# Batch 1's first transform stage on folded inputs, and the last quarter of w_in converted at the turn to the MLP

## The chip, the cores and the metric

The kernel runs on one core of a Trainium2 chip. The metric is the device time of one execution in microseconds (us). The core has five engines that run side by side, each through its own list of instructions in a fixed order: TensorE (PE; its weight loads are listed as PEld), VectorE (DVE), ScalarE (ACT), GpSimd (POOL) and SyncE (SP). DMAs are issued from the lists of SP and ScalarE.

## What is computed

For x of 8 batches x 3008 rows x 256 columns: a real FFT over the rows, a complex linear layer with bias on the 256 columns, a soft threshold of real and imaginary part apart, the inverse FFT, and then a two-layer MLP (256 to 2048 to 256) over all 24064 rows.

```python
X = np.fft.rfft(x, axis=1)                      # x: 8 x 3008 x 256
Yr = Xr @ w_r - Xi @ w_i + b_r
Yi = Xr @ w_i + Xi @ w_r + b_i
Yr = np.sign(Yr) * np.maximum(np.abs(Yr) - 0.01, 0.0)      # Yi alike
y = np.fft.irfft(Yr + 1j * Yi, n=3008, axis=1)
h = y.reshape(24064, 256) @ w_in                # w_in: 256 x 2048
out = np.maximum(0.01 * h, h) @ w_out           # w_out: 2048 x 256
```

The weights of the MLP arrive as 64-bit floats, read as pairs of 32-bit words.

## The kernel before

3008 is 47 x 64, so the FFT is done as products with small constant matrices. Per batch the work has these parts.

- Stage A (`fwd`): the 47-point transform. x comes as two halves, xa (row n) and xb (row -n). The cosine half needs xa + xb and the sine half xa - xb; making them is a fold. The columns are cut in seven groups c, six of 512 and one of 256; per group there are two results (h = 0, 1), which ScalarE copies from PSUM and which a DMA writes to `u_dram`. Batch 0 folds on VectorE, batches 2 to 7 fold on GpSimd (L245, L246). Batch 1 (`stage_a1`) doesn't fold: it makes each result from two products, with xa and with xb, using a third constant, the negated sine matrix (`fa32[:, 2]`); that is four products per group.
- The middle stage (`mid`): for 12 pairs j, a load of u, the 64-point transform (L343), a copy and sum ef (L347, L348), the linear layer (products into `pso` for the part kc, into `psf` for the rest), the bias sum on GpSimd (`kb = bias + kc`, L377, one buffer), then on VectorE t = psf + kb (L385), the clamp c (L386) and t - c (L387), then zf (four instructions on ScalarE, L391 and L395; for the last pair two of them on VectorE, L393), a product with zf (`stage_g`), a copy v and its write to `v_dram` (L415).
- The inverse (`inverse`): V is loaded (`vin`, L454), multiplied (L475), copied to odd (L478), combined on VectorE (L479, L481) and put in order in yc (L488). `forms` makes the sums of a seven-product scheme and splits each into a high and a low part (L500, L501) for one chunk of 512 rows, so an fp32-like product is three fast ones.
- The MLP (`moe`): 47 chunks x 8 steps q. A step has `moe_a` (products into `psh`, sums on VectorE, L538 to L541), `moe_b` (more products, L551 to L558 make g and split it into gh and gl) and, two steps later, `moe_o` (products with w_out into `pso`).

Both weights must be converted from 64-bit floats and split. w_in goes in quarters (`convert_win`, work tiles cva, cvq, ws), each with thirteen VectorE instructions, from `float64_parts` (L131 to L137) to the splits (L171, L172). w_out goes in eight chunks (`load_wout`; raw, then cva in tag "zf", L131 to L137 and L200 to L202); the first two raw loads are early, the other six use the two buffers "e" and "z" in turn. Step q of the first chunk of rows needs w_out chunk q two steps later.

The start of the program is: stage A of batch 0, quarters 0 and 1 of w_in, then the middle stage of batch 0 with quarters 2 and 3 of w_in and the x loads of batch 1 among it; then the turn: V of batch 0 is read back and inverted for the first chunk while TensorE does stage A of batch 1, five of its seven groups; the last two groups (c = 4, 5) come in the first MLP steps. From there on the MLP runs, with stage A and the middle stages of later batches in between.

The order of the instructions on each engine is made by a scheduler that goes by the order in which the program issues them and by a model of the engines. `tc.issue_after(x)` only says that an instruction is placed after x; it adds no wait by itself. Tiles with one tag share that tag's buffers in the order of their allocation, so a new tile waits for the last reader of the old one.

Of the kernel before, what the change touches and what calls it, by code (L numbers as in the profile page):

```python
# [8 lines left out]
F32 = mybir.dt.float32  # L9
# [11 lines left out]
P = 128  # L21
PA = NK1 * NG
# [8 lines left out]
def spectral_mlp_kernel(  # L31
# [125 lines left out]
    def convert_win(c):  # L157


        a, q, s = win_tmp  # L160
        float64_parts(win_raw[c], a, q)
        dve.tensor_add(a, a, q)
        a = a.rearrange("p (j q i m) -> p j q i m", j=NH, q=2, i=2)
        a11, a12, a21, a22 = (a[:, j, :, i] for i in range(2) for j in range(2))
        dve.tensor_add(s[:, 0], a21, a22)
        dve.tensor_sub(s[:, 2], a11, a21)
        dve.tensor_sub(s[:, 1], s[:, 0], a11)
        dve.tensor_sub(s[:, 3], a12, s[:, 1])
        hi, lo = (w[:, :, 2 * c:2 * c + 2] for w in consts["win"])
        for k, w in ((slice(0, 2), a[:, :, :, 0]), (2, a22), (slice(3, 7), s)):  # L170
            act.copy(hi[:, k], w)  # L171
            last = dve.tensor_sub(lo[:, k], w, hi[:, k].bitcast(F32))  # L172
        return last
# [36 lines left out]

    reads, written, turned, turning, thresholded = [], [], [], [], []
    NX = -(-NS // 2)
# [3 lines left out]
    def fwd(b):  # L216
# [5 lines left out]
        def load(c):  # L222
            cols = slice(2 * c * D, min(2 * c + 2, NS) * D)
            n = cols.stop - cols.start
            if b < NPRE:
                tag, bufs = (XT, XT1)[b][c]
                x2 = sb.tile([PA, 2, 2 * D], F32, name="xin", tag=tag, bufs=bufs)
                x_t[c] = [x2[:, h, :n] for h in range(2)]
            else:
                x_t[c] = [  # L230
                    sb.tile([PA, 2 * D], F32, name=f"xin{h}", tag="uv"[h], bufs=3 - h)[:, :n] for h in range(2)
                ]
# [25 lines left out]
        def stage_a(c, h):  # L258
# [9 lines left out]
            if b == 0:  # L268
                written.append(st)

        def stage_a1(c):

            n = x_t[c][0].shape[1]
            pas = [(bank("psf", 2) if c in (4, 5) else bank("psh", 4))[:PA, :n] for _ in range(2)]
            for h in range(2):
                with tc.issue_after(turning[NPAIR - 2].ins):
                    products(pas[h], [
                        (consts[f"fa{h}32"], (x_t[c][0],)), (consts[f"fa{2 * h}32"], (x_t[c][1],))])
            for h in range(2):
# [3 lines left out]
        if b == 1:  # L283
            for c in range(NX):
                load(c)
                yield 0
            for c in (0, 1, 2, 3, 6, 4, 5):
                stage_a1(c)
                yield 6 * x_t[c][0].shape[1]
# [22 lines left out]
    def mid(b):  # L312
# [49 lines left out]
        def proj(j):  # L362
# [4 lines left out]
            for dst, c, w in ((0, 2, "wr"), (0, 1, "wn"), (D, 0, "wd")):  # L367
# [5 lines left out]
                if c == 2:  # L373
                    kc = sb.tile([P, D], F32, name="kc", tag="kc")
                    act.copy(kc, ps_k[:, :D])  # L375
                    kb = sb.tile([P, 2, D], F32, name="kb", tag="kb", bufs=1)
                    pool.tensor_add(kb, bias, kc.unsqueeze(1).broadcast_to([P, 2, D]))  # L377
                if c:
# [263 lines left out]

    fa32 = sb.tile([PA, 3, PA], F32, name="fa32", tag="xi", bufs=1)
    for h in range(2):
        sync.dma_start(fa32[:, h], fa[h])
    for h in range(3):
        consts[f"fa{h}32"] = (fa32[:, h],)
# [14 lines left out]
        sb.tile([P, 4, 2, P], F32, name="ws", tag="yh"))  # L662
    act.mul(fa32[:, 2], fa32[:, 1], -1.0)
    convert_win(0)
# [16 lines left out]
    for i in range(1, 17):  # L681
        m0.to(i / 16)
        if i in (3, 8):
            convert_win(2 + i // 8)
        if 5 <= i < 12:
# [3 lines left out]
    m0.finish()  # L689
    fp.to(0.69)  # L690
    for p in due[0]:
# [4 lines left out]
    for _ in forms(0):  # L696
        pass
    next(wout)
    next(wout)
# [4 lines left out]
    for i, pos in enumerate(moe()):  # L704
        if i % 2 == 0 and len(converted) < NQ:
            with tc.issue_after(made[0].ins):
                next(wout, None)
        if i in (2, 4):
            with tc.issue_after(parted[0].ins), tc.issue_after(parted[1].ins):
                next(fp.gen)  # L710
        while cur + 1 < NB - 1 and pos >= (read[cur + 1] if cur >= 0 else 0):
# [115 lines left out]
```

## Time and profile before

| | |
|---|---|
| median of 3 runs | 2602.71 us (2602.45 to 2603.89) |
| the profiled execution | 2602.35 us, of which the span 2600.5 us |
| TensorE busy | 2537.5 us (98%) |
| VectorE busy | 1906.0 us (73%) |
| ScalarE busy | 1663.6 us (64%) |
| GpSimd busy | 252.3 us (10%) |
| granted TensorE clock, mean | 0.993 |

The profile gives, for one execution, every instruction with its start, its duration and the line of the kernel that issued it, and, in brackets, how long its engine was idle before it and what ended that. "L386" is line 386 of the kernel before; "out<-in" are its tiles. The span is the time from the first to the last instruction; the rest of the execution's time lies around it. The stage table sums busy time over stretches of the span; the chain of waits follows back from the last instruction to what released it each time; grouped rows give the count, the busy time in us, the mean in ns and the idle time before.

### The profile page before, as it was taken

How to read it: one execution, taken by the hardware profiler on the slowest of the kernel's cores; microseconds unless marked ns; L12 is line 12 of the kernel's file. 1: busy time of each engine (PE TensorE's matmuls, PEld its weight loads, DVE VectorE, ACT ScalarE, POOL GpSimd, SP SyncE). 2: the span in 40 equal slices, each digit the busy share in tenths (PEclk: the TensorE clock that was granted, in tenths of full speed). 3: DMA queues.
4: the chain of work that ended last, by engine and by line, in shares of the span. 5: the costliest groups of instructions: out<-in, count | busy, mean ns of one | idle time of the engine just before them, and what ended most of it. 6: DMA issues, size and time to landing. Idle time of an engine off the chain costs nothing.

```text
span 2600.5 us, 42617 instructions
## 1 busy us (share of the span) xinstructions
PE 2537.5 (98%) x16276; PEld 2278.2 (88%) x16276; DVE 1906.0 (73%) x3400; ACT 1663.6 (64%) x3172; POOL 252.3 (10%) x192
## 2 busy tenths in 40 slices
PE   6899999999999999999999999999999999999999
PEld 4579888999889998899988999889998889999988
DVE  7797777777777778777787777877777777767675
ACT  4667665766656666567666666566666667655554
POOL 1200121000110001100020000210002000000000
PEclk8999999999999999999999999999999999999999
DMA  8531123111221112211132111321113221100000
GB/s 260 161 93 57 45 74 90 52 48 46 82 81 50 41 45 86 78 52 45 40 94 71 49 49 37 104 65 50 50 34 102 65 58 48 43 17 32 9 17 17
DMA packets 119904, 165.12 MB, mean 63 GB/s; under 512 B 13597, under 2 KB 69909, under 8 KB 119701
## 3 DMA queue, kind: packets, MB, share of 16 engines
q1 hardware_dynamic: 79112, 115.54, 14.4%
q10 hardware_dynamic: 40589, 46.87, 7.1%
q8 instruction: 128, 2.10, 0.3%
q14 instruction: 75, 0.61, 0.1%
HBM read 86.60 MB, written 75.76 MB: 62 GB/s over the span
## 4 chain that ended last, share of the span: by engine, by line
PE 88%; DVE 3%; ACT 2%; DMA 1%; issue 1%; ACTq 0%; DVEq 0%
PE pso L571 37%; PE psh L92 34%; PE psf L78 11%; PE psf L475 3%; PE psf L343 3%; DMA u_dram<-xin 1%; DMA u<-u_dram 1%; DVE yl L501 1%; DVE gl L558 0%; DVE gf L552 0%; ACT gf L554 0%; ACT gh L556 0%; DVE yt L506 0%; DVE yc L507 0%; DVE gf L541 0%
## 5 line engine op out<-in xcount | busy, mean ns | idle before, releaser
L92 PE MATMUL psh<-yh,win_hi 128*128 128x256 f32 x2632 | 753.0, 286 | 14.9 <-DVE gf L541 11.5
L92 PE MATMUL psh<-yl,win_hi 128*128 128x256 f32 x2632 | 738.8, 281 | 0.6 <-DVE yl L501 0.5
L92 PE MATMUL psh<-yh,win_lo 128*128 128x256 f32 x2632 | 738.2, 280 | 0.0
L571 PE MATMUL pso<-gh,wout_hi 128*128 128x512 f32 x1504 | 593.9, 395 | 0.0
L571 PE MATMUL pso<-gl,wout_hi 128*128 128x512 f32 x1504 | 591.4, 393 | 0.5 <-DVE gl L558 0.5
L571 PE MATMUL pso<-gh,wout_lo 128*128 128x512 f32 x1504 | 590.4, 393 | 0.0
L558 DVE TENSOR_TENSOR gl<-gf,gh 128x1024 fp32r<-128x1024 f32 x376 | 470.3, 1251 | 91.5 <-ACT gh L556 89.6
L92 PEld LDWEIGHTS psh<-yh,win_hi 128*128 128x128 f32 x2632 | 497.2, 189 | 32.7 <-DVE gf L541 16.4
L92 PEld LDWEIGHTS psh<-yl,win_hi 128*128 128x128 f32 x2632 | 497.2, 189 | 12.4 <-DVE yl L501 1.0
L92 PEld LDWEIGHTS psh<-yh,win_lo 128*128 128x128 f32 x2632 | 496.8, 189 | 0.2
L552 DVE TENSOR_TENSOR gf<-psh,u 128x512 f32<-128x512 f32 x376 | 259.0, 689 | 256.3 <-PE psh L92 255.1
L556 ACT CAST gh<-gf 128x1024 fp32r<-128x1024 f32 x376 | 395.5, 1052 | 7.2
L554 ACT ACTIVATE gf<-gf 128x768 f32<-128x768 f32 x376 | 319.3, 849 | 50.8 <-DVE gf L552 48.8
L571 PEld LDWEIGHTS pso<-gl,wout_hi 128*128 128x128 f32 x1504 | 282.6, 188 | 62.7 <-DVE gl L558 1.0
L571 PEld LDWEIGHTS pso<-gh,wout_hi 128*128 128x128 f32 x1504 | 283.1, 188 | 46.6 <-ACT gh L556 0.4
L571 PEld LDWEIGHTS pso<-gh,wout_lo 128*128 128x128 f32 x1504 | 282.8, 188 | 44.7
L551 ACT ACTIVATE gf<-psh 128x256 f32<-128x256 f32 x376 | 145.0, 386 | 268.3 <-PE psh L92 245.8
L377 POOL TENSOR_TENSOR kb<-bias,kc 128x512 f32<-128x512 f32 x96 | 138.7, 1444 | 1607.0 <-ACT kc L375 1511.3
L537 ACT COPY p<-psh 128x256 f32<-128x256 f32 x376 | 139.5, 371 | 219.9 <-PE psh L92 219.2
L538 DVE TENSOR_TENSOR u<-psh,p 128x256 f32<-128x256 f32 x376 | 158.5, 422 | 103.9 <-ACT p L537 101.4
L540 DVE TENSOR_TENSOR gf<-psh,u 128x256 f32<-128x256 f32 x376 | 159.1, 423 | 29.6 <-PE psh L92 1.8
L541 DVE TENSOR_TENSOR gf<-psh,gf 128x256 f32<-128x256 f32 x376 | 159.0, 423 | 9.0
(126 smaller groups left out, 3252.3 us busy)
## 6 DMA issues: line engine op xcount, KB each, us to landing
u<-u_dram SPq DMA_DIRECT2D x192, 128.0 KB, 2.7
v_dram<-v ACTq DMA_DIRECT2D x192, 128.0 KB, 2.4
out_dram<-ob SPq DMA_DIRECT2D x94, 256.0 KB, 2.1
vin<-v_dram SPq DMA_DIRECT2D x96, 240.0 KB, 3.4
xin<-x_dram SPq DMA_DIRECT2D x90, 240.0 KB, 2.9
u_dram<-xin ACTq DMA_DIRECT2D x72, 240.0 KB, 2.4
u_dram<-xin SPq DMA_DIRECT2D x24, 240.0 KB, 4.8
raw<-w_out_dram SPq DMA_DIRECT2D x8, 512.0 KB, 5.3
```

Of the source, the lines that this page charges most:

```text
L78: last = nc.tensor.matmul(dst, a, b, start=(i == 0), stop=(i == len(terms) - 1))
L92: mlp[:] = [nc.tensor.matmul(dst, a, b, start=start and i == 0, stop=i == 2, skip_group_check=True)]
L537: act.copy(p1, b1[:, lo])
L538: dve.tensor_add(u2, b1[:, hi], p1)
L540: dve.tensor_add(g[:, 3], b2[:, hi], u2)
L541: dve.tensor_add(g[:, 3], b2[:, lo], g[:, 3])
L551: act.activation(g[:, 0], b1[:, lo], AF.Prelu, alpha=SLOPE)
L552: dve.tensor_add(g[:, 1:3], b2.rearrange("p (k n) -> p k n", k=2), u2.unsqueeze(1).broadcast_to([P, 2, HT]))
L554: act.activation(g[:, 1:4], g[:, 1:4], AF.Prelu, alpha=SLOPE)
L556: cp = act.copy(gh, g)
L558: parted[:] = [cp, dve.tensor_sub(gl, g, gh.bitcast(F32))]
L571: mlp[:] = [nc.tensor.matmul(po, a[:, f, s], r[:, i], start=(f == 0 and j == 0), stop=(f == NF - 1 and j == 2),)]
```

## The change

Batch 1 now folds too, on GpSimd, in place (`fold1`): per group, xs = xa + xb goes into a spare half tile (the first spare is a third part of group 4's tile; after that the freed xb of the group before), and xa becomes xa - xb. So `stage_a1` has two products per group instead of four, 14 in all instead of 28, and the negated matrix and the ScalarE instruction that made it go. The folds are issued after the x loads, each placed after a bias sum of batch 0's middle stage: group 0 after the seventh, group 1 after the eighth, and so on, groups 5 and 6 after the twelfth.

All seven groups of stage A of batch 1 are issued before the first forms, in the order 0 to 6, and groups 4 and 5 use the PSUM buffers `pso` instead of `psf`. Quarter 3 of w_in is converted after the middle stage of batch 0 is issued, with its own work tile cva in tag "e"; quarter 2 is issued one sixteenth later than before. One `next(wout)` ahead of the MLP is dropped, so one chunk of w_out less is converted there and one more in the MLP's first steps.

```diff
@@ convert_win
         a, q, s = win_tmp
+        if c == 3:
+            a = sb.tile([P, NH * NIN], F32, name="cva", tag="e", bufs=1)
         float64_parts(win_raw[c], a, q)
@@ fwd, load
-                x2 = sb.tile([PA, 2, 2 * D], F32, name="xin", tag=tag, bufs=bufs)
+                spare = b == 1 and c == 4
+                x2 = sb.tile([PA, 3 if spare else 2, 2 * D], F32, name="xin", tag=tag, bufs=bufs)
                 x_t[c] = [x2[:, h, :n] for h in range(2)]
+                if b == 1:
+                    s_t[c] = x2[:, 1]
+                if spare:
+                    s_t[-1] = x2[:, 2]
@@ fwd
+        def fold1(c):
+            xa, xb = x_t[c]
+            n = xa.shape[1]
+            xs = s_t[-1][:, :n]
+            s_t[-1] = s_t.pop(c)
+            pool.tensor_add(xs, xa, xb)
+            pool.tensor_sub(xa, xa, xb)
+            x_t[c] = [xs, xa]
...
-            pas = [(bank("psf", 2) if c in (4, 5) else bank("psh", 4))[:PA, :n] for _ in range(2)]
+            pas = [(bank("pso", 2) if c in (4, 5) else bank("psh", 4))[:PA, :n] for _ in range(2)]
             for h in range(2):
                 with tc.issue_after(turning[NPAIR - 2].ins):
-                    products(pas[h], [
-                        (consts[f"fa{h}32"], (x_t[c][0],)), (consts[f"fa{2 * h}32"], (x_t[c][1],))])
+                    products(pas[h], [(consts[f"fa{h}32"], (x_t[c][h],))])
...
-            for c in (0, 1, 2, 3, 6, 4, 5):
+            for c in range(NX):
+                with tc.issue_after(biased[min(NPAIR - NX + 1 + c, NPAIR - 1)].ins):
+                    fold1(c)
+            for c in range(NX):
                 stage_a1(c)
@@ mid, proj
-                    pool.tensor_add(kb, bias, kc.unsqueeze(1).broadcast_to([P, 2, D]))
+                    add = pool.tensor_add(kb, bias, kc.unsqueeze(1).broadcast_to([P, 2, D]))
+                    if b == 0:
+                        biased.append(add)
@@ the start of the program
-    act.mul(fa32[:, 2], fa32[:, 1], -1.0)
...
-        if i in (3, 8):
-            convert_win(2 + i // 8)
+        if i == 4:
+            convert_win(2)
...
     m0.finish()
-    fp.to(0.69)
+    convert_win(3)
+    fp.finish()
...
     next(wout)
-    next(wout)
...
-        if i in (2, 4):
-            with tc.issue_after(parted[0].ins), tc.issue_after(parted[1].ins):
-                next(fp.gen)
```

What this makes of the order is shown at three places. Line numbers after the change are up to 21 higher than before (the bias sum is L396, t, c and t - c are L406 to L408, vin is L475).

GpSimd at the end of batch 0's middle stage, before: kb is a bias sum; the last row is the first one of batch 1.

```order
L377 TENSOR_TENSOR kb_632<-bias_249,kc_630 128x512
L377 TENSOR_TENSOR kb_669<-bias_249,kc_667 128x512
L377 TENSOR_TENSOR kb_707<-bias_249,kc_705 128x512
L317 MEMSET zero_1381 48x256
L377 TENSOR_TENSOR kb_734<-bias_249,kc_732 128x512
L377 TENSOR_TENSOR kb_1491<-bias_249,kc_1489 128x512
```

The same place after, from the tenth sum (kb_650) to the twelfth (kb_715) and the folds behind it; xin are the halves of x.

```order
L396 TENSOR_TENSOR kb_650<-bias_248,kc_648 128x512
L285 TENSOR_TENSOR xin_492<-xin_492 120x512
L284 TENSOR_TENSOR xin_492<-xin_524 120x512
L285 TENSOR_TENSOR xin_524<-xin_524 120x512
L396 TENSOR_TENSOR kb_688<-bias_248,kc_686 128x512
L284 TENSOR_TENSOR xin_524<-xin_554 120x512
L336 MEMSET zero_1381 48x256
L396 TENSOR_TENSOR kb_715<-bias_248,kc_713 128x512
L285 TENSOR_TENSOR xin_554<-xin_554 120x512
L284 TENSOR_TENSOR xin_554<-xin_577 120x512
L285 TENSOR_TENSOR xin_577<-xin_577 120x512
L284 TENSOR_TENSOR xin_577<-xin_615 120x256
```

Nine fold instructions now stand between the seventh and the twelfth sum, and five behind the twelfth (the last of them isn't shown).

VectorE at the last pair, before: t, c, t - c and the two instructions on zf, then the first of w_out.

```order
L385 TENSOR_TENSOR t_740<-psf_729,kb_734 128x512
L386 TENSOR_SCALAR c_741<-t_740 128x512
L387 TENSOR_TENSOR t_740<-t_740,c_741 128x512
L393 TENSOR_SCALAR zf_232<-t_740,sign_111 64x256 x2
L133 TENSOR_SCALAR cva_888<-cva_888 128x512
```

The same place after; cva_748 is quarter 3 of w_in.

```order
L133 TENSOR_SCALAR cva_748<-cva_748 128x1024
L406 TENSOR_TENSOR t_721<-psf_710,kb_715 128x512
L134 TENSOR_SCALAR cva_748<-cva_748 128x1024
L407 TENSOR_SCALAR c_722<-t_721 128x512
L135 SCALAR_TENSOR_TENSOR cva_748<-win_raw_251,cva_748 128x1024
L408 TENSOR_TENSOR t_721<-t_721,c_722 128x512
L136 TENSOR_SCALAR win_raw_251<-cva_748 128x1024
L414 TENSOR_SCALAR zf_231<-t_721,sign_111 64x256 x2
L137 TENSOR_TENSOR cvq_181<-cvq_181,win_raw_251 128x1024
```

Four instructions of the quarter now stand among those of the last pair.

SP in the turn, before: the four loads of V for the first chunk, two loads of w_out (raw) and the writes of stage A.

```order
L454 DMA vin_817<-v_dram_226 120x512
L454 DMA vin_820<-v_dram_226 120x512
L454 DMA vin_817<-v_dram_226 120x512
L454 DMA vin_820<-v_dram_226 120x512
L186 DMA raw_933<-w_out_dram 128x2x512
L281 DMA u_dram_431<-xin_432 120x512
L186 DMA raw_935<-w_out_dram 128x2x512
L281 DMA u_dram_431<-xin_432 120x512
```

The same place after, without the two writes of stage A that stand ahead of these rows.

```order
L475 DMA vin_837<-v_dram_225 120x512
L297 DMA u_dram_430<-xin_554 120x512
L297 DMA u_dram_430<-xin_431 120x512
L475 DMA vin_837<-v_dram_225 120x512
L475 DMA vin_840<-v_dram_225 120x512
L297 DMA u_dram_430<-xin_431 120x512
L297 DMA u_dram_430<-xin_554 120x512
L475 DMA vin_840<-v_dram_225 120x512
L297 DMA u_dram_430<-xin_577 120x512
L297 DMA u_dram_430<-xin_454 120x512 x2
L297 DMA u_dram_430<-xin_492 120x512
L188 DMA raw_993<-w_out_dram 128x2x512
```

The loads of V now stand among the writes of stage A, and the third and fourth load of w_out (raw_993 and the row behind it) behind eight of those after the first load of V.

More of the change, by code (lines that the diff above doesn't have):

```diff
@@ L209, in spectral_mlp_kernel @@
     v_dram = {}
[L211 removed]
+    reads, written, turned, turning, thresholded, biased = [], [], [], [], [], []
     NX = -(-NS // 2)
@@ L640, in spectral_mlp_kernel @@
     FWD = NS * 6 * D
-    fa32 = sb.tile([PA, 3, PA], F32, name="fa32", tag="xi", bufs=1)
+    fa32 = sb.tile([PA, 2, PA], F32, name="fa32", tag="xi", bufs=1)
     for h in range(2):
         sync.dma_start(fa32[:, h], fa[h])
-    for h in range(3):
+    for h in range(2):
         consts[f"fa{h}32"] = (fa32[:, h],)
```

## The prediction

> **What bounds the kernel now.** I read the table by stage first. Its columns are the stretch, its length, then busy time and instructions of TensorE, its weight loads, VectorE, ScalarE and GpSimd, the granted clock, and the DMA share and rate.
>
> ```profile
> 73.90:95.60 21.70, 19.41 (x98) 14.89 (x97) 20.48 (x30) 17.92 (x39) 8.16 (x5) 1.00 0.45 120
> 95.60:108.70 13.10, 8.93 (x22) 4.07 (x22) 7.29 (x13) 7.24 (x16) 3.01 (x3) 0.75 0.31 75
> 108.70:134.45 25.75, 25.63 (x88) 13.81 (x86) 14.35 (x31) 15.26 (x32) 0.00 (x0) 0.93 0.73 214
> 134.45:160.35 25.90, 20.68 (x120) 16.35 (x119) 24.16 (x50) 17.28 (x33) 0.00 (x0) 1.00 0.39 119
> 160.35:300.00 139.65, 139.30 (x923) 127.57 (x924) 108.20 (x203) 96.92 (x190) 10.95 (x8) 0.99 0.18 52
> ```
>
> From 160.35 us on TensorE is busy 139.30 of 139.65 us: what the change is worth is how much earlier or later that point comes. Before it stand three stages. The second half of batch 0's middle stage (73.9 to 95.6) has VectorE at 20.48 of 21.70 and TensorE at 19.41. The turn (108.7 to 134.45) has VectorE little over half busy. The first MLP steps (134.45 to 160.35) have VectorE at 24.16 of 25.90. Then the chain of waits at its turning point:
>
> ```profile
> 158.23 1.13 DVE gl L558
> 159.36 0.60 DVE cvq L137
> 159.96 0.35 DVE gf L541
> 160.35 3.88 PE psh L92 x18
> 164.23 2.75 PE pso L571 x12
> 173.14 2.52 PE psh L92 x21
> ```
>
> Until 160.3 the chain runs on VectorE, where a w_out instruction (L137) stands among the MLP's; from 160.35 on it stays on TensorE. The marker I carry through the sum is this L541, the fourth one (MLP step 3).
>
> **TensorE's halved stage A of batch 1.**
>
> ```profile
> L78 PE MATMUL psh<-xin,fa 120*120 120x512 f32 x32 | 16.5, 660 | 0.0
> L78 PE MATMUL psf<-xin,fa 120*120 120x512 f32 x16 | 7.3, 597 | 0.1
> L78 PE MATMUL psh<-xin,fa 120*120 120x256 f32 x8 | 1.9, 380 | 0.0
> ```
>
> 28 products (two instructions each) become 14, so (16.5 + 7.3 + 1.9) / 2 = 12.9 us of TensorE go. On the path I price this at nothing: the 7.3 lies in the VectorE-bound steps, and the rest fills the time in which TensorE waits for the turn's DMAs. If VectorE weren't late there, up to 12.9 would count.
>
> **The fourth quarter leaves the middle stage.** VectorE's instructions on cva, and the last one, on ws alone (same columns, VectorE only):
>
> ```profile
> 73.90:95.70 21.80, 7.88 (x11) 1.00 0.45 120
> 93.30:95.70 2.40, 2.30 (x1) 1.00 0.27 65
> ```
>
> 7.88 + 2.30 = 10.2 us, in which two instructions were held up once each by GpSimd (next part, 1.08 us): 8.0 us of VectorE leave this stage.
>
> **Fourteen GpSimd instructions come in.** What GpSimd costs VectorE, and what one fold takes:
>
> ```profile
> 70.80 0.41 DVE L386 TENSOR_SCALAR c<-t 128x512 f32<-128x512 f32 x1
> 76.25 1.58 POOL L377 TENSOR_TENSOR kb<-bias,kc 128x512 f32<-128x512 f32 x1 [1.29 <-DVE t L385]
> 76.63 1.49 DVE L386 TENSOR_SCALAR c<-t 128x512 f32<-128x512 f32 x1
> 83.20 2.86 POOL L377 TENSOR_TENSOR kb<-bias,kc 128x512 f32<-128x512 f32 x1 [5.36 <-ACT kc L375]
> 83.72 1.22 DVE L162 TENSOR_TENSOR cva<-cva,cvq 128x1024 f32<-128x1024 f32 x1
> 86.09 0.69 DVE L385 TENSOR_TENSOR t<-psf,kb 128x512 f32<-128x512 f32 x1 [1.16 <-POOL kb L377]
> L246 POOL TENSOR_TENSOR xin<-xin,xin 120x512 f32<-120x512 f32 x36 | 52.6, 1462 | 2.8
> L246 POOL TENSOR_TENSOR xin<-xin,xin 120x256 f32<-120x256 f32 x6 | 4.4, 741 | 0.5
> ```
>
> The same clamp (L386) takes 0.41 us alone and 1.49 when a bias sum runs: a GpSimd instruction costs the VectorE instruction behind it 1.08 us. The sum at 83.20 shows the other outcome: it took 2.86 us and VectorE's 1.22 us instruction beside it took its usual time, so there GpSimd gave way. The two exclude each other. A 512-wide fold takes about as long as a bias sum, so I take 1.08 for it, and 0.5 for a 256-wide one (741 / 1462 of it); the ends are 0 (always in VectorE's gaps) and 1.46. The Trainium skill (SBUF — State Buffer, "Who interferes with whom") says that the shared port pair is an exclusive lock held for the whole instruction, and that an instruction of VectorE with one input in SBUF, outside its two-port modes, stays clear. This speaks against the change; the trace agrees on the exclusion, but shows 1.08 lost where the page's whole instruction would be about 1.46, which over nine folds would add 3.4 us.
>
> No wait instruction is added: the gate only fixes the order. But each later bias sum now queues behind folds on GpSimd, and VectorE's t (L385) waits for it. Nine folds stand between the seventh and the last bias sum: 9 x 1.08 = 9.7 us come, 8.0 go, and L133 of the quarter stands before the last t (0.6). VectorE's own gaps (1.16 us before the t at 86.09, and 1.86 before the last t, shown below) take some 1 of it. So the last t moves from 102.35 to about 103.7; ends 99 (folds all in gaps; TensorE's 2.3 us of idle time from 73.9 to 95.6 and some of the next stage then bound it) and 105.5.
>
> Behind it the chain to the last product of this stage now shares VectorE with three more instructions of the quarter and five folds:
>
> ```profile
> L134 DVE TENSOR_SCALAR cva<-cva 128x1024 uint32<-128x1024 uint32 x1 | 0.7, 677 | 0.0
> L135 DVE SCALAR_TENSOR_TENSOR cva<-win_raw,cva 128x1024 uint32<-128x1024 uint32 x1 | 1.2, 1212 | 0.0
> L136 DVE TENSOR_SCALAR win_raw<-cva 128x1024 uint32<-128x1024 uint32 x1 | 0.7, 679 | 0.0
> 102.35 0.69 DVE L385 TENSOR_TENSOR t<-psf,kb 128x512 f32<-128x512 f32 x1 [1.86 <-POOL kb L377]
> 104.26 0.72 DVE L393 TENSOR_SCALAR zf<-t,sign 64x256 f32<-64x256 f32 x2
> 106.64 2.08 PE L78 MATMUL psh<-zf,w 128*128 128x512 f32 x2 [1.66 <-ACT zf L391]
> ```
>
> From t to the end of zf is 104.98 - 102.35 = 2.6 us; the three add 2.6, less 0.3 of overlap; three wide and two narrow folds add 3 x 1.08 + 2 x 0.5 = 4.2. The last zf product starts at 103.7 + 2.6 + 2.3 + 4.2 + 0.1 = 112.9 instead of 106.64: +6.3. Ends: -0.6 (folds free) and +8.
>
> **The turn.**
>
> ```profile
> 109.37 1.24 ACTq L415 DMA_DIRECT2D v_dram<-v  x2
> 111.90 1.69 SPq L454 DMA_DIRECT2D vin<-v_dram  x4
> 113.67 0.40 SPq L186 DMA_DIRECT2D raw<-w_out_dram  x1
> 117.36 0.61 PE L475 MATMUL psf<-ga,vin 120*128 120x128 f32 x4
> 120.61 0.68 ACT L131 ACTIVATE cvq<-raw 128x512 f32<-128x512 uint32 x1 [3.32 <-DMA raw<-w_out_dram]
> 124.80 0.37 ACT L478 COPY odd<-psf 128x240 f32<-128x240 f32 x1
> 130.53 0.35 ACT L478 COPY odd<-psf 128x240 f32<-128x240 f32 x1
> 134.45 0.42 DVE L133 TENSOR_SCALAR cva<-cva 128x512 f32<-128x512 f32 x1
> ```
>
> The inverse (L475) starts 10.7 us after the last zf product. Now the last v_dram writes queue on ScalarE behind two casts of the quarter that wait for VectorE (some 1.1 us), and the four vin loads on SP stand among four or more u_dram writes (0.3 us each, 1.2): 112.9 + 10.7 + 2.3 = 125.9 instead of 117.36. But most of that is covered: ScalarE took the first odd copy only at 124.80, 7 us after its product, since a w_out activation in front of it waited for its DMA until 120.6. So the first odd moves to 126.3 only. What is late next is the same wait in a new place: the third and fourth w_out loads are queued behind the u_dram writes, at about 125.0, and landed 6.9 us after issue here (113.67 to 120.61); ScalarE's activation on them now stands between the third and fourth odd copies. 125.0 + 6.9 + 0.6 + 0.5 gives 133.0 for the fourth odd instead of 130.53. The split behind it shifts alike: the first steps begin at 137.0 instead of 134.45, +2.5; ends -5 (with the folds free) and +4.5.
>
> VectorE's work on the quarter (8 us) and one w_out chunk lies in these 10.7 us of waiting; if that cover went, it would stand before the first steps in full.
>
> **The first steps.** Up to the marker, VectorE now does one more inverse (two instructions) and five more of the second chunk's forms (two narrow, three wide), but two instructions fewer of w_out and one gl fewer: 4 x 0.35 + 3 x 0.60 - (0.35 + 0.60) - 1.13 = +1.1. One gap of VectorE in this stretch comes from batch 1's output, whose tiles the forms take over; ScalarE's cast waited for its write, and VectorE for the cast:
>
> ```profile
> 153.41 0.41 ACT L500 CAST yh<-yc 128x256 fp32r<-128x256 f32 x1 [2.33 <-DMA u_dram<-xin]
> 153.85 0.42 DVE L501 TENSOR_TENSOR yl<-yc,yh 128x256 fp32r<-128x256 f32 x1 [1.29 <-ACT yh L500]
> ```
>
> With stage A of batch 1 done inside the turn that wait goes; of VectorE's 1.29 us I count 0.8, other waits taking the rest. Marker: +2.5 + 1.1 - 0.8 = +2.8. Behind it VectorE still has 4.3 us more of w_out than before (one more chunk, 0.35 x 3 + 0.60 x 4 = 3.4, and the 0.9 above). Per step VectorE then needs 3.4 for w_out and about 2.7 for the MLP, TensorE 2.5 + 2.75 = 5.2: 0.9 short over some three and a half steps, 3.2 at most, mostly absorbed, since the forms are already done and two products of the output lie between a step's sums and their use; I take 0.8, ends 0 and 3.2. On SP the last four w_out loads, each waiting for a converted chunk, now stand ahead of batch 1's u loads, so its middle stage starts later; TensorE's total doesn't change by that, and I price it at nothing as long as no V of batch 1 is due; if it is, TensorE shows a gap. Sum: +3.6 us on the profiled execution's 2602.35 us, giving 2605.9 (its span is 2600.5; the 1.85 around it stay); the median of the runs shown, 2602.71, is 0.4 above it, inside the range. At nothing I cost the third fa32 plane (ScalarE waits at that time anyway) and the pso buffers (idle until the MLP's first output).
>
> **The rivals.** (1) The last pair decides in full (slower). ScalarE now has the eleventh pair's kc copy behind the tenth's four zf copies, so that pair's bias sum waits for a clamp that folds hold up. Then the last t is at 105.5, the last zf product at 114.7 (+8), and with +4.5 at the first steps, +0.3 and the full 3.2 the run ends 8 us later: 2610.4. It decides from a last zf product later than about 114. For it: the clamp at 76.63 and the 2.30 us on ws were held, each by one sum. Against: the two gaps of VectorE.
> (2) GpSimd gives way, as at 83.20 (faster). The last zf product is at 106, the loads of w_out land at 124, the steps begin 5 us earlier, TensorE has stage A's half less to do, and 5 - 0.3 - 0.8 + 1.8 (the 18 products at 160.35 took 3.88 us, at full clock some 2.1) makes it 5.7 earlier: 2596.7. For it: the sum at 83.20, and gaps of 1.16 and 1.86 us, each nearly a fold long. Against: the clamp at 76.63, held though VectorE was busy without a break.
> That the change doesn't do what it says is no rival: the orders shown above have the folds, and TensorE's has 14 products. In every case the steady part is re-ordered a little on all engines, which I take as 1 to 2 us of either sign.
>
> **How the numbers follow.** 0.2%, about what a measurement of this kernel can tell from no change, is 5.2 us. My forecast, +3.6, lies inside: 0.54. Rival 1 has 0.28, rival 2 has 0.18. The range reaches to both: 2596.5 to 2611.0.
>
> **What would show it.** Right: clamps and quarter instructions on VectorE of 1.5 us and more from 77 to 113; a last zf product near 113; ScalarE waiting for w_out between odd copies near 131; the marker near 163. Wrong: a last zf product before 108, or folds that lengthen while VectorE's instructions don't (rival 2); a marker after 165 (rival 1); or TensorE with gaps long after 180 that it hasn't now.

## The result, and the profile after

| | before | after |
|---|---|---|
| median of the runs, us | 2602.70 (2602.45 to 2603.89) | 2634.70 (2632.98 to 2638.55) |
| the profiled execution, us | 2602.35 (span 2600.5) | 2638.55 (span 2636.7) |
| TensorE busy, us | 2537.5 | 2555.7 |
| VectorE busy, us | 1906.0 | 1914.8 |
| GpSimd busy, us | 252.3 | 271.6 |
| granted TensorE clock, mean | 0.993 | 0.986 |

The ratio is 1.0124, 95% interval 1.0107 to 1.0142: 32.0 us slower. That lies far outside the range. TensorE is busy for 18 us more, although 12.9 us of products were taken out.

First, where on the way the time is lost. These are DMA issues of the kernel before that write the output of a chunk of 512 rows: the last write of the second chunk, the pair of the seventh, and the last of all.

```profile
257.55 0.37 SPq L577 DMA_DIRECT2D out_dram<-ob  x1
533.32 0.92 SPq L577 DMA_DIRECT2D out_dram<-ob  x2
2597.69 0.33 SPq L577 DMA_DIRECT2D out_dram<-ob  x1
```

The same three places after the change (the first row is a pair, its second write 0.5 us behind the first; the second row is the second write alone).

```profile
267.93 0.89 SPq L598 DMA_DIRECT2D out_dram<-ob  x2
555.75 0.37 SPq L598 DMA_DIRECT2D out_dram<-ob  x1
2633.89 0.33 SPq L598 DMA_DIRECT2D out_dram<-ob  x1
```

The second write of the pairs taken each time, the delay is 11 us after two chunks, 22 after seven and 36 at the end (36.2 between the two profiled executions, 32.0 between the medians). So there are three losses: one at the start, one in the next five chunks, and a creeping one of 14 us over the other 40 chunks, in which the kernel does exactly the same work. The stage table after, over nearly the same stretches as in the prediction:

```profile
73.90:95.60 21.70, 18.44 (x87) 13.99 (x86) 14.88 (x17) 14.04 (x31) 14.11 (x10) 0.92 0.46 115
95.60:120.00 24.40, 16.04 (x40) 8.59 (x39) 21.88 (x26) 13.66 (x28) 15.92 (x13) 0.82 0.31 72
134.45:160.35 25.90, 14.98 (x72) 14.03 (x73) 20.87 (x45) 14.88 (x32) 0.00 (x0) 0.67 0.33 110
160.35:300.00 139.65, 134.47 (x870) 121.94 (x869) 108.55 (x202) 92.54 (x179) 10.49 (x7) 0.99 0.19 54
```

In the first MLP steps (134.45 to 160.35) TensorE was busy for 20.68 us at full clock before; now it is 14.98 at a clock of 0.67. Each gap of 1.59 us and more there has a stretch at half clock that begins inside it or within 0.8 us behind it: a product of L92 then takes 0.41 us instead of 0.28. The Trainium skill (TensorE: Matmul & The Clock Gate, "Part 1: The HAM clock gate") says that TensorE falls to half its clock after an idle window of about 3.4 us and climbs back after a busy one; the trace agrees in the length, the half-clock stretches within the span last 3.41 us or a multiple of it. It doesn't agree that a whole idle window is needed: three stretches start at 148.63, 155.46 and 165.70 us, where the longest gaps are 1.93, 1.59 and 2.30 us.

The last pair, VectorE and the product that waits for it:

```profile
107.82 0.68 DVE L406 TENSOR_TENSOR t<-psf,kb 128x512 f32<-128x512 f32 x1
108.42 1.15 DVE L134 TENSOR_SCALAR cva<-cva 128x1024 uint32<-128x1024 uint32 x1
109.49 1.48 DVE L407 TENSOR_SCALAR c<-t 128x512 f32<-128x512 f32 x1
110.90 1.75 DVE L135 SCALAR_TENSOR_TENSOR cva<-win_raw,cva 128x1024 uint32<-128x1024 uint32 x1
112.57 1.21 DVE L408 TENSOR_TENSOR t<-t,c 128x512 f32<-128x512 f32 x1
115.27 2.05 PE L78 MATMUL psh<-zf,w 128*128 128x512 f32 x2 [2.83 <-DVE zf L414]
134.89 0.66 ACT L131 ACTIVATE cvq<-raw 128x512 f32<-128x512 uint32 x1 [2.24 <-DMA raw<-w_out_dram]
135.92 0.35 ACT L499 COPY odd<-psf 128x240 f32<-128x240 f32 x1
```

Clamp (1.48), t - c (1.21) and the quarter's instructions are held up one by one by folds, as forecast (t itself, at its usual 0.68, isn't), and the w_out wait stands between the third and fourth odd copies. A part of the chain of waits behind that:

```profile
131.96 0.69 PE psf L496 x5
132.65 7.60 DMA vin<-v_dram
140.39 0.76 PE psf L496 x2
...
153.76 0.97 ACT gh L577
154.73 3.56 DMA raw<-w_out_dram
158.32 0.33 ACT cvq L131
```

New in the chain are a load of V for the second chunk (L496 is the inverse), on which TensorE waits 7.3 us in MLP step 0, behind its first three products, and a load of w_out that SP issues at 154.73, 16.7 us later than the same load before (138.04). Last, the groups of the MLP's first products, before and then after (x2632 each, columns busy us, mean ns):

```profile
L92 PE MATMUL psh<-yh,win_hi 128*128 128x256 f32 x2632 | 753.0, 286 | 14.9 <-DVE gf L541 11.5
L92 PE MATMUL psh<-yl,win_hi 128*128 128x256 f32 x2632 | 738.8, 281 | 0.6 <-DVE yl L501 0.5
L92 PE MATMUL psh<-yh,win_lo 128*128 128x256 f32 x2632 | 738.2, 280 | 0.0
```

```profile
L92 PE MATMUL psh<-yh,win_hi 128*128 128x256 f32 x2632 | 759.4, 289 | 17.5 <-DVE gf L562 13.8
L92 PE MATMUL psh<-yl,win_hi 128*128 128x256 f32 x2632 | 746.5, 284 | 2.7 <-DVE yl L522 2.7
L92 PE MATMUL psh<-yh,win_lo 128*128 128x256 f32 x2632 | 748.2, 284 | 0.0
```

In the mean all three groups of L92, 7896 products, became 3 to 4 ns slower, also the one that waits for nothing. From start to start (products whose next one starts within 160 ns, at full clock, behind the 54th product with w_out) the mean is 117.1 ns before and 119.3 after: 2.2 x 7,500 = 16 us. That is the creeping loss. Besides the order of the instructions around them, one thing that the change alters for them is where the tiles lie: fa32 lost its third plane, 480 bytes a partition, and with its slot every work tile behind it moved down by 416 bytes, while the MLP's weights win_hi and win_lo, in front of it, stayed.

### The profile page after: what moved, and what is told of

Its sections match the earlier page's. It is cut to its first block, busy times and chain, and to the rows that moved or that the text cites. A ratio compares the mean times of both kernels' runs of the same rounds, so it can differ in the third digit from the quotient of the medians.

```text
span 2636.7 us, 42589 instructions
## 1 busy us (share of the span) xinstructions
PE 2555.7 (97%) x16248; PEld 2300.5 (87%) x16248; DVE 1914.8 (73%) x3400; ACT 1663.9 (63%) x3171; POOL 271.6 (10%) x206
## 4 chain that ended last, share of the span: by engine, by line
PE 86%; DVE 5%; DMA 3%; ACT 3%; issue 2%; POOL 1%; SPq 0%; ACTq 0%; DVEq 0%; POOLq 0%
PE pso L592 36%; PE psh L92 33%; PE psf L78 11%; PE psf L496 3%; PE psf L362 2%; DMA u<-u_dram 1%; DMA u_dram<-xin 1%; DVE gl L579 1%; PE psh L78 1%; DVE yl L522 1%; DMA xin<-x_dram 0%; ACT gh L577 0%; DVE t L406 0%; DVE gf L573 0%; ACT zf L416 0%
## 5 line engine op out<-in xcount | busy, mean ns | idle before, releaser
L92 PE MATMUL psh<-yh,win_hi 128*128 128x256 f32 x2632 | 759.4, 289 | 17.5 <-DVE gf L562 13.8
L92 PE MATMUL psh<-yl,win_hi 128*128 128x256 f32 x2632 | 746.5, 284 | 2.7 <-DVE yl L522 2.7
L92 PE MATMUL psh<-yh,win_lo 128*128 128x256 f32 x2632 | 748.2, 284 | 0.0
L592 PE MATMUL pso<-gh,wout_hi 128*128 128x512 f32 x1504 | 594.3, 395 | 0.0
L592 PE MATMUL pso<-gh,wout_lo 128*128 128x512 f32 x1504 | 590.9, 393 | 0.0
L592 PE MATMUL pso<-gl,wout_hi 128*128 128x512 f32 x1504 | 589.7, 392 | 0.5 <-DVE gl L579 0.5
L92 PEld LDWEIGHTS psh<-yh,win_hi 128*128 128x128 f32 x2632 | 500.3, 190 | 34.4 <-DVE gf L562 19.3
L92 PEld LDWEIGHTS psh<-yl,win_hi 128*128 128x128 f32 x2632 | 500.1, 190 | 14.4 <-DVE yl L522 3.3
L92 PEld LDWEIGHTS psh<-yh,win_lo 128*128 128x128 f32 x2632 | 499.8, 190 | 0.3
L592 PEld LDWEIGHTS pso<-gl,wout_hi 128*128 128x128 f32 x1504 | 283.0, 188 | 63.1 <-DVE gl L579 1.0
L592 PEld LDWEIGHTS pso<-gh,wout_hi 128*128 128x128 f32 x1504 | 283.7, 189 | 47.2 <-ACT gh L577 0.4
L592 PEld LDWEIGHTS pso<-gh,wout_lo 128*128 128x128 f32 x1504 | 283.4, 188 | 43.8
L396 POOL TENSOR_TENSOR kb<-bias,kc 128x512 f32<-128x512 f32 x96 | 136.8, 1425 | 1616.8 <-ACT kc L394 1521.6
```

What stands on the lines that cost most here:

```text
L92: mlp[:] = [nc.tensor.matmul(dst, a, b, start=start and i == 0, stop=i == 2, skip_group_check=True)]
L592: mlp[:] = [nc.tensor.matmul(po, a[:, f, s], r[:, i], start=(f == 0 and j == 0), stop=(f == NF - 1 and j == 2),)]
```

## Experiments

Times are differences of medians to the kernel before in the same set of runs. "Wide" means the changed kernel with the third plane kept in the tile.

| run | what | ratio (95% interval) | us | L92, start to start, ns |
|---|---|---|---|---|
| e1_after_wide | wide | 1.0075 (1.006 to 1.009) | +19.3 | 117.1 |
| e2_before_shift | before, work tiles +32 bytes | 0.9973 (0.9962 to 0.9984) | -6.6 | 116.9 |
| e3_before_const64 | before, constants +32, work tiles +64 | 0.997 (0.9959 to 0.9981) | -7.5 | 116.9 |
| e4_late_groups | wide, groups 4, 5 late | 1.0037 (1.0023 to 1.0051) | +9.1 | 117.1 |
| e5_late_wout | e4, w_out chunk kept ahead | 1.0018 (1.0008 to 1.0027) | +4.9 | |
| e6_late_quarter | e4, quarter in the middle stage | 1.0063 (1.0048 to 1.0078) | +16.0 | |
| e7_late_nofold | e4, no folds | 1.0036 (1.0022 to 1.005) | +9.0 | |
| e8_fold_alone | before, folds alone | 1.0033 (1.0021 to 1.0045) | +8.1 | |
| e9_const_moved | after, constants and work tiles +416 | 1.0122 (1.0107 to 1.0138) | +31.2 | 119.3 |
| e10_before_96 | before, work tiles +96 | 1.0058 (1.0043 to 1.0073) | +15.3 | 119.3 |
| e11_wout_ahead | wide, w_out chunk kept ahead | 1.003 (1.0019 to 1.0042) | +8.1 | 117.1 |
| e12_after_shift | after, at the place of e2 | 1.0044 (1.0027 to 1.0061) | +11.7 | 116.9 |
| e13_before_64 | before, work tiles +64 | 1.0062 (1.0047 to 1.0077) | +16.7 | 119.6 |
| e14_before_128 | before, work tiles +128 | 1.0024 (1.0014 to 1.0033) | +6.4 | 118.0 |
| e15_before_224 | before, work tiles +224 | 1.006 (1.0043 to 1.0077) | +15.6 | 119.6 |
| e16_folds_last | e5, folds behind the last sum | 1.0032 (1.0021 to 1.0043) | +8.2 | |
| e17_quarter_alone | e5, no folds | 1.0011 (1.0002 to 1.0021) | +2.9 | |
| e18_quarter_shift | e17, work tiles +32 | 0.9988 (0.9978 to 0.9997) | -3.8 | |

**The place of the tiles.** The third plane back, unused; the order of all engines is that of the changed kernel:

```diff
-    fa32 = sb.tile([PA, 2, PA], F32, name="fa32", tag="xi", bufs=1)
+    fa32 = sb.tile([PA, 3, PA], F32, name="fa32", tag="xi", bufs=1)
```

> The changed kernel with the third plane of fa32 kept in its tile (nobody writes or reads it), so that every work tile behind it lies 416 bytes further up, at a multiple of 64 bytes as in the kernel before; the order of all engines is the same as the changed kernel's. Theory 1 (the place of the tiles): the 7896 products of L92 go back from a mean of 289/284/284 to 286/281/281 ns, about 2.2 ns each from start to start, 16 us in all: 2617 to 2621 us. Theory 2 (the slower products come from the new order of the steady part): nothing changes, 2633 to 2636.

12.7 us came back (+32.0 to +19.3), and L92 has the speed of before:

```profile
L92 PE MATMUL psh<-yh,win_hi 128*128 128x256 f32 x2632 | 753.4, 286 | 18.6 <-DVE gf L562 14.2
L92 PE MATMUL psh<-yl,win_hi 128*128 128x256 f32 x2632 | 739.1, 281 | 2.8 <-DVE yl L522 2.8
L92 PE MATMUL psh<-yh,win_lo 128*128 128x256 f32 x2632 | 738.8, 281 | 0.0
```

So the place costs about 13 of the 32 us. My rule for it, a place at 32 above a multiple of 64, was tried on the kernel before:

```diff
-    fa32 = sb.tile([PA, 3, PA], F32, name="fa32", tag="xi", bufs=1)
+    fa32 = sb.tile([PA, 3 * PA + 8], F32, name="fa32", tag="xi", bufs=1)[:, :3 * PA].rearrange("p (a b) -> p a b", a=3)
```

> The kernel before with fa32's tile 32 bytes wider, nothing else: the work tiles lie 32 bytes above a multiple of 64, as in the changed kernel; the order is that of before. Theory 1: the products of L92 slow down to 289/284/284 ns, 2602.7 + 16 = 2615 to 2621 us, without any change of the work. Theory 2: 2602 to 2604.

It fell: this place is faster than that of before, by 6.6 us. Both sides moved (the line above and a wider tile in front of the constants):

```diff
-    sign = const.tile([P, NK1 + NPAIR], F32, name="sign")
+    sign = const.tile([P, 48], F32, name="sign")[:, :NK1 + NPAIR]
```

> The kernel before with the constants moved by 32 bytes (the sign tile wider) and the work tiles again at multiples of 64: now the MLP's weights win_hi and win_lo lie at a multiple of 64 too, where before they lay 32 above one. If only the moving side yh, yl counts: 2602 to 2604. If it counts that weights and moving tiles lie differently by 32 modulo 64: slower by about 16. If every tile counts by itself: faster, 2590 to 2600.

The third time came out, but not what it stood for: the speed is that of e2, 116.9 ns. In both the work tiles lie 32 bytes further from the weights than before, at different places of their own. For the changed kernel the same question, with the distance left as it is (-416) and the work tiles put back to where they lie before:

```diff
-    sign = const.tile([P, NK1 + NPAIR], F32, name="sign")
+    sign = const.tile([P, 144], F32, name="sign")[:, :NK1 + NPAIR]
```

> The changed kernel with the sign tile 416 bytes wider: all constants behind it (the MLP's weights win_hi, win_lo among them) move up by 416 bytes, and the work tiles with them, to exactly the places that they have in the kernel before; the distance from win to yh and yl stays that of the changed kernel. Same order. If the places of the work tiles themselves set the speed of L92: 286/281/281 ns and 2620 to 2624 us. If the distance between the weights and the moving tiles does: 289/284/284 ns, 2633 to 2637.

```profile
L92 PE MATMUL psh<-yh,win_hi 128*128 128x256 f32 x2632 | 760.0, 289 | 16.3 <-DVE gf L562 12.6
L92 PE MATMUL psh<-yl,win_hi 128*128 128x256 f32 x2632 | 746.9, 284 | 2.7 <-DVE yl L522 2.7
L92 PE MATMUL psh<-yh,win_lo 128*128 128x256 f32 x2632 | 748.8, 285 | 0.0
```

Still slow: what counts is the distance between the constants, the MLP's weights among them, and the work tiles, the moving yh and yl among them, and not the place of the work tiles. That it is these two that matter is argued from what L92 reads; all work tiles moved together in every run. The changed kernel at e2's distance (the tile 3 * PA + 8 wide):

> The changed kernel with fa32's tile 1472 bytes wide, so that its work tiles lie where they lie in the kernel before with 32 bytes more (2596.1 us, 6.6 under before). Same order as the changed kernel. If the places act alike in both kernels: 6 to 7 us under the changed kernel with the third plane alone, 2614 to 2617 us. If the gain of that place hung on the order of before: 2620 to 2624.

It gained 7.6 us on e1, so the distance acts alike in both orders. For its rule, the kernel before with 96 (3 * PA + 24), 64 (+ 16), 128 (+ 32) and 224 bytes (+ 56):

> The kernel before with fa32's tile 96 bytes wider, so that the work tiles lie 96 bytes higher; 96 is what the changed kernel's shift of -416 leaves modulo 128, 256 and 512. If the effect repeats with one of these: L92 at 289/284/284 ns, 2614 to 2619 us. If it doesn't, it is one of larger distances: 2595 to 2604.

> The kernel before with its work tiles 64 bytes higher. Shifts of 0, 32 and 96 bytes gave L92 at 117.1, 116.9 and 119.3 ns from start to start. If the price follows the distance in steps of 32 within 128 bytes, 64 has a value of its own between the others': 2596 to 2618 us, any of it new; if only an odd multiple of 96 is bad, 117 ns and 2595 to 2603.

> The kernel before with its work tiles 128 bytes higher. If the effect of the place repeats every 128 bytes: the speed of before, 2601 to 2604 us, L92 at 286/281/280 ns. If its period is 256 or 512: another value, as likely 2596 or 2617.

> The kernel before with its work tiles 224 bytes higher, 96 modulo 128 as in the changed kernel (-416). Period of 128: slow as with 96, 2614 to 2619 us, L92 at 288/284/284 ns. Period of 256 or 512: 2595 to 2604.

Shifts of 64, 96 and 224 are slow, 0 and 32 fast, 128 in between with 118.0 ns (and +6.4 us), so a plain period of 128 bytes isn't it; 96 and -416, which are 512 apart, give the same 119.3. The rule stays open. A pure move of 96 bytes costs 15.3 us; all that the change does to the work costs 19.3.

**Groups and w_out.** The late groups restored in the wide kernel:

```diff
-    fp.finish()
+    fp.to(0.69)
...
+        if i in (2, 4):
+            with tc.issue_after(parted[0].ins), tc.issue_after(parted[1].ins):
+                next(fp.gen)
...
-            for c in range(NX):
+            for c in (0, 1, 2, 3, 6, 4, 5):
                 stage_a1(c)
...
-            pas = [(bank("pso", 2) if c in (4, 5) else bank("psh", 4))[:PA, :n] for _ in range(2)]
+            pas = [(bank("psf", 2) if c in (4, 5) else bank("psh", 4))[:PA, :n] for _ in range(2)]
```

> The changed kernel with the third plane kept, and with the last two groups of stage A of batch 1 (c = 4, 5) again in the first MLP steps and in psf, as before; folds, the quarter at the turn and w_out as changed. On TensorE the two inverse products of the second chunk then stand behind step 0 instead of in front of it. Order theory (TensorE's wait of 7.3 us on the second chunk's V in front of step 0 is what delayed the first steps): 7 to 10 us less than the kernel with the third plane alone, 2608 to 2613. The prediction's own theory (the late last pair sets the delay, +3.6): the delay of the first steps stays, 2616 to 2621.

The size came out (10.2 us less than e1), the reason didn't. TensorE no longer waits for the second chunk's V in step 0, but the write that ends the second chunk isn't earlier (266.96 against 264.75 in e1). The gain lies in the five chunks behind it. With the late groups, the chunk of w_out ahead again:

```diff
     next(wout)
+    next(wout)
```

> The kernel with the third plane kept and the late groups (2611.75 us, 9.1 over before), and the dropped chunk of w_out converted ahead of the MLP again, as before. Theory W (every w_out chunk is converted one step later, so VectorE makes the inputs of the steps late; TensorE's 4.5 us gap at 171.69 in that kernel is this): the gap goes, 2605 to 2608 us. Theory Z (the delay is that of the first steps, which the last pair, held up by folds and the quarter, passes on): one more chunk in front of the steps, no gain, 2611 to 2614.

4.2 us less; the gap of 4.52 us at 171.69 shrinks to one of 1.61 (at 171.79). The row in e4, and the w_out instructions among the forms that made VectorE late for it:

```profile
171.69 0.47 PE L92 MATMUL psh<-yh,win_hi 128*128 128x256 f32 x1 [4.52 <-DVE gf L562]
```

```profile
167.34 0.68 DVE L137 TENSOR_TENSOR cvq<-cvq,raw 128x512 f32<-128x512 f32 x1
167.94 0.68 DVE L203 TENSOR_TENSOR cva<-cva,wout_hi 128x512 f32<-128x512 f32 x1
...
170.61 0.68 DVE L204 TENSOR_TENSOR wout_lo<-cva,cvq 128x512 fp32r<-128x512 f32 x1
171.22 0.42 DVE L562 TENSOR_TENSOR gf<-psh,gf 128x256 f32<-128x256 f32 x1
```

The same edit in the wide kernel, all seven groups ahead:

> The changed kernel with the third plane kept and all seven groups ahead (2622.0 us), and the dropped chunk of w_out converted ahead of the MLP again. Theory G (the loss in chunks 2 to 6 comes from batch 1's middle stage, which is placed behind the last w_out conversion, and starts too late for its V): that stage starts a step earlier, 2610 to 2614 us. Theory H (the loss belongs to the seven groups ahead and the second chunk's inverse in front of step 0): only the 4.3 us that the same edit gave with the late groups, 2616 to 2619.

11.2 us less, though in this kernel the second chunk's inverse still stands in step 0, behind its first three products (wait of 5.5 us). TensorE from the end of the second chunk to the end of the seventh, in e1 and in e11:

```profile
264.75:550.35 285.60, 278.46 (x1803) 0.99 0.23 65
```

```profile
265.10:541.25 276.15, 272.47 (x1780) 1.00 0.23 65
```

In e1 these five chunks hold some twenty TensorE instructions more (14 of them of middle stages, done earlier in e11), 3.5 us more of waiting, and a half-clock stretch; together 9.4 us. SP's first load of u for that middle stage is issued at 162.15 before and at 183.52 after; 179.74 in e1 and 175.91 in e11:

```profile
162.15 1.23 SPq L329 DMA_DIRECT2D u<-u_dram  x2
```

```profile
183.52 0.58 SPq L348 DMA_DIRECT2D u<-u_dram  x1
```

The program places this stage behind the last w_out conversion (`tc.issue_after(converted[-1].ins)`), and each later w_out load waits until the chunk two before it, whose buffer it takes, is converted. So the dropped `next(wout)` pushes batch 1's middle stage back (its u loads by 3.8 us, e11 to e1), and so do the groups ahead (1.9, e4 to e1). Either edit alone takes most of the loss away: with all groups ahead the chunk of w_out is worth 11.2 us, with late groups 4.2. That the late start itself is what costs the time is argued, not shown: in e4 the u loads start at 177.82, only 1.9 us earlier than in e1, and these five chunks take 275.95 us, no longer than before (276.33); in e5 they start 11.9 us later than before and the chunks take 276.99.

**Folds and quarter.** The quarter back in the middle stage (in e4: the lines of the change undone), the folds left out (four products a group again), and the folds alone in the kernel before:

> The kernel with the third plane kept and the late groups (2611.75 us), with quarters 2 and 3 of w_in converted in the middle stage, where they were before. The prediction's sum (the quarter's 8.0 us of VectorE count in the middle stage, where folds are added): its last zf product moves later than 115.05 by 6 to 8 us and the run gets 2 to 6 us longer, 2614 to 2618. Theory Q (the quarter costs more in the turn, in front of the first forms and among the last pair, than in the middle stage): 2604 to 2609, with the last zf product before 113.

> The kernel with the third plane kept and the late groups (2611.75 us), without the folds: batch 1's stage A has four products per group again. Theory F (each fold holds VectorE up by 1.08 us, and that is what delays the last pair): the last zf product goes from 115.05 to about 106 to 108, the inverse starts 6 to 8 us earlier; TensorE has 12.9 us more to do, of which 7.3 would lie in the first steps; 2606 to 2610. If the folds cost nothing: 2611 to 2616 with the last zf product at 114 to 116.

> The kernel before, with the folds on GpSimd and the halved stage A alone; quarter 3, w_out and the last two groups stay where they were. Theory F: the nine folds in the middle stage add 9.7 us to VectorE there with nothing taken away, last zf product at 115 to 118, first steps 4 to 8 us later, less what the halved products give back: 2606 to 2611 us. Theory Z2 (the delay comes from the quarter and w_out, the folds are taken up by gaps): 2597 to 2603.

The last zf product in e4, e6, e7 and e8:

```profile
115.05 2.05 PE L78 MATMUL psh<-zf,w 128*128 128x512 f32 x2 [3.97 <-DVE zf L414]
```

```profile
118.26 2.07 PE L78 MATMUL psh<-zf,w 128*128 128x512 f32 x2 [2.18 <-ACT zf L410]
```

```profile
109.22 2.07 PE L78 MATMUL psh<-zf,w 128*128 128x512 f32 x2 [2.45 <-ACT zf L410]
```

```profile
116.84 2.07 PE L78 MATMUL psh<-zf,w 128*128 128x512 f32 x2 [2.15 <-ACT zf L410]
```

Without folds it comes 5.8 us earlier, and the run still takes the same time (+9.0 and +9.1): TensorE's 12.9 us of products are back, some of them in the first steps. The quarter put back costs 6.9 us (e6), in sign as the forecast's sum had it; but the last zf product moved by only 3.2 us, where 6 to 8 were expected, so the way from the one to the other isn't shown. The folds, with the halved stage A, cost 8.1 in the kernel before, with the zf product 10.2 us later, as the first theory had it. Then the folds moved behind the last sum, in e5:

```diff
-                with tc.issue_after(biased[min(NPAIR - NX + 1 + c, NPAIR - 1)].ins):
+                with tc.issue_after(biased[NPAIR - 1].ins):
```

> The changed kernel with the third plane kept, the late groups and the chunk of w_out kept (2607.45 us), and all fourteen folds gated behind the last bias sum instead of between the sums. If the folds among the sums cause the rest of the loss (4.9 us): the last zf product comes at 108 to 111 instead of 115.6, and the run at 2601 to 2605. If the folds in the turn then hold up the quarter, the forms and stage A's writes, behind which V and w_out are loaded: 2606 to 2612, with the first step's products no earlier than 138.

```profile
117.24 2.05 PE L78 MATMUL psh<-zf,w 128*128 128x512 f32 x2 [9.03 <-DVE zf L414]
```

Worse by 3.3 us: now all of them stand beside the last clamp and t - c, and TensorE waits 9 us for zf. Last, e5 without folds, which is the kernel before with the quarter at the turn alone, and the same at the good place:

> The kernel before with quarter 3 of w_in converted at the turn, and nothing else of the change: no folds, the late groups, both chunks of w_out ahead, the third plane. If the folds make the 4.9 us that are left in the same kernel with folds (2607.45 us): 2599 to 2603, the last zf product at 108 to 110. If the quarter at the turn makes them: 2605 to 2609, the first step's products at 137 or later though the last zf product is early.

> The same with the work tiles 32 bytes higher, the place that made the kernel before 6.6 us faster. If the place acts here as there: 6 to 9 us under the kernel with the quarter alone; with a quarter that costs nothing that is 2592 to 2597, at the level of the kernel before at that place (2596.07).

The last zf product is at 109.05, as the first expectation had it, and the run at +2.9, a time of the second: the quarter at the turn makes the larger part of what was left. Some 2 us of e5's 4.9 come with the folds, less than the two intervals together can tell from zero, and 2.9 with the quarter. At the good place it is 2599.93, above the kernel before at that place (2596.07). Of all that was run, e2 and e3 alone beat both kernels clearly; they hold nothing of the change.

Put together, one path from after to before: the place 12.7 (after to e1), the w_out chunk 11.2 (e1 to e11), the late groups 3.2 (e11 to e5), the folds with the halved stage A 2.0 (e5 to e17), the quarter 2.9. The sum is 32.0 because each step starts where the one before ends; in another order the shares differ (the late groups first are worth 10.2, the w_out chunk then 4.2). The steps of 3.2 and 2.0 lie within the intervals of the runs on either side.

## Why the prediction was wrong

Its chain up to the first steps held within 3 us. The last zf product was forecast at 112.9; it came at 115.27, and at 113.37 in e1, which has the same order and was 1.9 us ahead at the seventh t already (76.2 against 78.1 us), in front of the folds. The inverse was to start at 125.9; that it came at 126.08 is luck, since from the last zf product to it there were 10.8 us as before, not 2.3 more (e1: 122.85). The fourth odd copy was to come at 133.0 behind the wait for w_out (135.92, in e1 133.65). The folds do hold up VectorE, and the quarter's way out of the middle stage pays for part of it. No run halves stage A without folding; the two together brought nothing in e4 (against e7) and cost 8.1 us in e8. With the place, the w_out chunk and the late groups put back, the kernel stands at +4.9 us (e5, 2607.45), where the forecast without its 0.8 for that chunk had +2.8. Rival 1's condition came true (a last zf product after 114), and its time nearly does when the other losses are put back: 4.8 without its 3.2 for the w_out chunk against e5's +4.9, 8.0 with it against e4's +9.1. Its mechanism isn't shown by that: in e7 the last zf product comes 5.8 us earlier than in e4 and the run gains nothing, though there the 12.9 us of products are back too. Rival 2 (GpSimd gives way) is refuted by the clamp and the t - c above.

Three steps failed.

- "At nothing I cost the third fa32 plane": the ScalarE instruction was indeed free; the freed space wasn't. It moved the work tiles, and that costs 12.7 us (after to e1, the same order), where the sum had nothing and the forecast's 1 to 2 us for the steady part spoke of a re-ordering. Nothing in the order or the trace of before shows it; the tile sizes in the diff do.
- "I take 0.8, ends 0 and 3.2" for VectorE's shortfall with one more w_out chunk. It was 4.2 with the late groups and 11.2 with all groups ahead. The price went by VectorE's busy time. With the late groups the rows at 167 to 171 us show what it left out: every later conversion comes a step later, among the forms, and TensorE waits for them. Why the same chunk costs 11.2 with all groups ahead stays open.
- Batch 1's later middle stage: "I price it at nothing as long as no V of batch 1 is due; if it is, TensorE shows a gap". The u loads start 21.4 us later, and the five chunks take 11.0 us longer (287.34 against 276.33), of which e11 gives back 9.4 in the wide kernel; nothing was the wrong price. The sign that it named didn't come: batch 1's first V is loaded right behind the last write of V before and after (369.8 and 388.3 us), and from 369 to 468 us TensorE has no gap above 0.25 us after the change. The waits that e1 has and e11 hasn't stand later, at 476 and 478 us on forms and at 530 on a middle stage's eh. How the edits lead there stays open. The marker, the fourth L541, came at 169.48 us instead of 159.88, 9.6 later where 2.8 was forecast. It stood too early to measure the loss by: in e4 it came at 160.37, and the run was still 9.1 us over.

The pso buffers were costed at nothing too, and the groups ahead only at the VectorE instructions that move with them. The scheduler put the second chunk's inverse ahead of nearly all of step 0 (with psf free for it, which is the likely reason), where its V, queued behind stage A's writes on SP, wasn't there for 7.3 us. e4 shows that this wait alone isn't what delays the second chunk's end: VectorE is late at that point anyway.

## What to carry to other kernels

When an edit changes the size of an on-chip tile, look at which tiles move with it, and compare the kernel with a padded one before judging the edit; here a pure move of 32 to 96 bytes was worth from -6.6 to +16.7 us of 2600. A step that is "only later" has to be followed to what is placed behind it: the wait list of the next stage, and the queue that its loads share. Taking products off an engine that waits brought no gain here, with the folds that it took, and a helper instruction on GpSimd is paid for by VectorE where the two meet, as at the clamps here (0.41 us alone, 1.48 beside a fold).

## What the runs showed of the hardware

- The pace of a 128x256 product followed the distance in SBUF between the constants, its weights among them, and the work tiles, its moving tile among them: 116.9, 117.1, 118.0, 119.3 and 119.6 ns for shifts of 32, 0, 128, 96 and 64 bytes (224 as 64), with an unchanged order, and 119.3 at -416 whether the work tiles or both sides had moved. The Trainium skill (SBUF — State Buffer, "Who interferes with whom") gives TensorE two independent read ports, for the moving operand and for the weights, and says that it never waits on anyone; in these runs the pace moved by up to 2.7 ns a product with nothing but the place of tiles. That the two reads collide is argued, not shown.
- The longer products with w_out (L592, 128x512) hardly changed: 230.1 ns before, 229.7 after, 229.3 at +32. Their weights lie among the work tiles, like the gh and gl that they read, so no run here changes the distance between the two, and none tells whether this shape would follow it.
- In the first steps one gap of 7.3 us and four of 0.65 to 1.93 went with a granted clock of 0.67 over 26 us.
